# A Fourier mixing and GEGLU kernel on one core: the lone token's products in a tile of their own, and one buffer for folded x

## The chip, the cores and the metric

The kernel runs on one core of a Trainium2 chip. The metric is the device time of one execution in microseconds (us). The engines are named as in the profile: PE is TensorE's matmuls and PEld its weight loads, DVE is VectorE, ACT is ScalarE, POOL is GpSimd, SP is SyncE. Each engine works through its own queue in order; semaphores tie the queues together.

## The reference

```python
def reference(x, w_gate, w_val, w_out):       # x: (8, 3008, 256), d_ff = 1536
    X = np.fft.fft(np.fft.fft(x, axis=1), axis=2).real    # per batch
    X = X.reshape(8 * 3008, 256)
    g = X @ w_gate
    gelu = 0.5 * g * (1.0 + erf(g / sqrt(2)))
    return (gelu * (X @ w_val)) @ w_out
```

All inputs and the output are float32.

## The kernel before

The real part of the transform is built from an even and an odd part over the features, and token t and token T - t share their work. So of the 3008 tokens of a batch only the columns 0 to 1504 (`NCOL` = 1505) are worked through, and each column gives two tokens: a "plus" one and a mirrored "minus" one. Two tokens have no partner of their own, token 0 and token T/2. The latter is called the lone token here.

**Transform.** For each of 8 batches, x comes in by three loads into the tiles `xins`. `fold_x` adds and subtracts mirrored features into the tile xf, 24 pairs of columns wide, in pieces of two columns (two TENSOR_TENSOR and one copy, in the main loop on POOL). `a_step(b, k)` multiplies columns 2k and 2k+1 of xf with the tile G on TensorE. The result goes through DRAM (`z_write`, `z_read`) into Ap, and `b_steps` makes Y from it, with the even part in Y[:, 0] and the odd part in Y[:, 1]. Before, there are two xf tiles, and batch b uses number b % 2.

**Layer 1.** The columns are taken in three chunks, `CH = [(1024, NCOL - 1024), (0, 512), (512, 512)]`, and each chunk in 12 units of 128 features of the hidden layer. So a batch has 36 units, and u counts units over all batches (288). In unit u TensorE makes the gate and value products in PSUM (`ps_g`, `ps_v`). ACT makes gelu of the plus and minus gates (`glp`, `glm`). DVE makes `ev` from each value bank, and for each pair of units the plus products of h (`h<-glp,ps_v`, in `val_odd`), followed by `dv`. POOL makes the minus products of h (`h<-glm,dv`, in `minus`), 128x1024 at a time. In program order the products of a pair are written one unit after its second unit was opened.

**The h buffers.** Each chunk of each batch has an h tile of 12 x 1024 columns, and there are two buffers for it, taken in turn. Chunk 2 of a batch takes the buffer that chunk 0 of that batch had.

**Layer 2.** When a chunk is done, `l2_steps` queues its products with w_out (`ps_o`, TensorE), by windows of 128 tokens. In every following unit, `second` issues eight of them (six in some). `windows` says which columns of h belong to which token rows. When it is called for chunk 0, it also copies 64 left-over columns of h into hx and CW on POOL.

**The lone token.** Its plus products stand in column 960 of chunk 0's h. Its place in the output belongs to a window of chunk 1, column 1023. When the last unit of chunk 1 is done, the line ahead of `l2q += l2_steps(pb, pi)` copies the column from one h tile to the other, on POOL. At that time the buffer's next tenant, chunk 2, has been opened; its first plus products come two units later.

**Order.** Everything is issued in the order in which the Python code runs, engine by engine (`keep_in_program_order`). A unit runs: `val_even`, `gate_minus` and `val_odd` of the unit before, `gate_plus`, steps of the next batch's transform in between (`fills`), `minus`, `fold_x` for the batch after next (for the next one in batch 0's first units), `a_step` for the next batch, and at last `second`. In units 0 to 11 of a batch, `a_step(b + 1, k)` runs in unit k; `fold_x(b + 2, ...)` writes columns 2k and 2k+1 from unit 2k + 5 on. In batch 0 both follow plans of their own (`a_first`, and units 13 to 35).

A tile that is written anew waits for the last readers and writers of what it overwrites; the framework puts in these waits.

Of the kernel before, what the change touches and what calls it, by code (L numbers as in the profile page):

```python
# [10 lines left out]
BF16 = mybir.dt.bfloat16  # L11
# [16 lines left out]
def _sub(base: bass.AP, free_pattern, free_offset, part_start=0, part_num=None):  # L28
    p_step, p_count = base.ap[0]
    if part_num is None:  # L30
        part_num = p_count - part_start
    pat = [[p_step, part_num]] + [list(x) for x in free_pattern]
    off = base.offset + part_start * p_step + free_offset
    return ap_replace(base, ap=pat, offset=off)
# [3 lines left out]
def kernel(  # L38
# [21 lines left out]
    sync, vec, act, pool, pe = (  # L60
        _InOrder(tc, e) for e in (nc.sync, nc.vector, nc.scalar, nc.gpsimd, nc.tensor))
# [5 lines left out]
    HJ = 24  # L67
    NG = 32
    NCH = C // 128
    NFC = F // 128  # L70
# [5 lines left out]
    const_pool = ctx.enter_context(tc.tile_pool(name="const", bufs=1))  # L76
# [20 lines left out]
    NQs = [const_pool.tile([128, YW], BF16, name=f"nq{i}") for i in range(2)]  # L97
    HXF = NFC - NCH * 2
    hx = const_pool.tile([128, HXF, 128], BF16)
    xf_bufs = [const_pool.tile([128, HJ, 2, 128], BF16, name=f"xf{i}") for i in range(2)]  # L100

    Ap = const_pool.tile([128, NG, C], BF16)

# [24 lines left out]
    def S1_tile():  # L128
        return work.tile([128, HJ, C], BF16, tag="S1", bufs=1, name="S1")
# [58 lines left out]
    def ps_o():  # L188
        return psum.tile([128, 512], FP32, tag="o", bufs=1, name="ps_o")

    def ps_d():
        return psum.tile([128, 512], FP32, tag="d", bufs=1, name="ps_d")
# [16 lines left out]

    def fold_x(b, i, eng, a0=0, an=8, other=None):  # L210
        xt = xins[i]
        xf = xf_bufs[b % 2]
        o0 = (8 * i + a0) * C
        lo = _sub(xt, [[C, an], [1, 127]], a0 * C + 1)
        hi = _sub(xt, [[C, an], [-1, 127]], a0 * C + 255)
        ea = _sub(xf, [[C, an], [1, 127]], o0 + 1)
        od = _sub(xf, [[C, an], [1, 127]], o0 + 129)
        eng.tensor_tensor(ea, lo, hi, op=ALU.add)
        eng.tensor_tensor(od, lo, hi, op=ALU.subtract)
        (other or eng).tensor_copy(  # L220
            _sub(xf, [[C, an], [128, 2]], o0), _sub(xt, [[C, an], [128, 2]], a0 * C))
# [239 lines left out]

    def a_step(b, k):

        xf = xf_bufs[b % 2]
        if "S1" not in st[b]:
            st[b]["S1"] = S1_tile()
        S1 = st[b]["S1"]
        if b == 0:
            ps = (ps_g, ps_vh, ps_o if k % 8 < 4 else ps_d, ps_vh)[k % 4]()
        else:  # L470
            ps = ps_o() if b == 1 and k % 2 and 1 < k < 10 else ps_d()
        for i in range(2):
            jj = 2 * k + i
            on_half(ps, pe.matmul(
                ps[:, i * C : (i + 1) * C], G[:, jj, :], _sub(xf, [[1, C]], jj * C),
                start=True, stop=True))
        dst = _sub(S1, [[1, 2 * C]], 2 * k * C)
        if b == 0 and k % 2 == 0 and k >= 8 or b == 1 and k in (0, 3, 5, 7, 9):
            return on_half(ps, vec.tensor_copy(dst, ps))
        return on_half(ps, act.activation(dst, ps, AF.Copy))  # L480
# [92 lines left out]
    hs, banks, duos = {}, {}, {}  # L573
# [93 lines left out]
    def windows(b, ci):  # L667
        h = hs[(b, ci)]
        c0, n = CH[ci]
        m0, nb = c0 // 32, n // 32  # L670
        ps = [plus_rows(b, m0 + i) for i in range(nb)]
        ms = [minus_rows(b, m0 + nb - 1 - i) for i in range(nb)]
        blocks = ps + ms if n == 512 else ms + ps
        order = range(8) if n == 512 else (4, 5, 6, 0, 1, 2, 3)
        out = [(h, 128 * w, blocks[4 * w : 4 * w + 4], None) for w in order]
        if c0 == 0:
            out[-1] = out[-1][:3] + (b * T + T // 2,)
        if len(blocks) % 4:
            left = blocks[-2:]
            o = 64 * (b % 2)  # L680
            pool.tensor_copy(hx[:, :, o : o + 64], h[:, :HXF, 896:960])
            pool.tensor_copy(_sub(CW, [[128, NCH * 2], [1, 64]], o), h[:, HXF:, 896:960])
            if b % 2:
                out.append((None, 0, st[b - 1]["left"] + left, None))
            else:
                st[b]["left"] = left
        return out
# [161 lines left out]
    for u in range(NU + 2):  # L849
        b, i = divmod(u, PER)  # L850
        fills = []
        tail = None
        held = False
        if u < NU:
            open_unit(u)
            loads = (0, 14, 19) if b else (8, 12, 18)
            if i in loads and b + 2 < B:
                load_x(b + 2, loads.index(i))
            if b + 1 < B:
                for what in plan[min(b, 1)].get(i, ()):  # L860
                    if what == "n":
                        tail = lambda b=b: n_step(b + 1)
                        continue
                    eo, q, lo, hi = what
                    if lo == 0:
                        held = True
                        st[b + 1]["cur"] = b_steps(b + 1, eo, q)
                    fills += st[b + 1]["cur"][0][lo:hi]
                    if hi == 8:
                        tail = st[b + 1]["cur"][1]  # L870

        def fill(most=2):
            for _ in range(most):
                if fills:
                    fills.pop(0)()

        def second(n):
            for _ in range(n):
                if l2q:
                    l2q.pop(0)()  # L880

        if u == 0:
            r = banks[0]
            r["pg"] = ps_g()
            layer1(r, r["pv"], WE, 1, 0, r["n"], True)
            layer1(r, r["pg"], WE, 0, 0, r["n"], True)
            layer1(r, r["pg"], WOP, 0, 1, r["n"], False)
            layer1(r, r["pv"], WOP, 1, 1, r["n"], False)
            for e in later_evacs:
                e()  # L890
            n_first(0)
            act.activation(r["glp"][:, : r["n"]], r["pg"][:, : r["n"]], AF.Gelu)
            plus(r)
        elif u < NU:
            val_even(u)
            if not held:
                fill()
        if 0 < u <= NU:
            gate_minus(u - 1)
            if not held:  # L900
                fill()
        early = 0 < u <= NU and banks[u - 1]["kd"]
        if early:
            val_odd(u - 1)
        if 0 < u < NU:
            gate_plus(u, fill)
            if banks[u]["kd"] == 0:
                plus(banks[u])
        if 0 < u <= NU and not early:
            val_odd(u - 1)  # L910
        while fills:
            fill()
        if tail:
            tail()
        if 0 < u <= NU:
            minus(u - 1)
        if u < NU:
            if b + 1 < B and i == (19 if b else 21):
                n_turn(b + 1)
            if b + 1 < B and i == 30:  # L920
                n_read(b + 1)
        if u < NU:
            if b == 0:
                for e in extra.get(i, ()):
                    e()
                if i < 12:
                    fold_x(1, i // 4, pool, i % 4 * 2, 2)
            if i % 2 and b + 2 < B:
                j = i - 1
                if b:  # L930
                    f, fp = next((j - o, n) for n, o, z in ((0, 4, 18), (1, 18, 28), (2, 28, 36)) if j < z)
                else:
                    fp, f = divmod(j - 12, 8)
                if 0 <= f < 8 and fp >= 0:
                    fold_x(b + 2, fp, pool, f, 2)
            if b + 1 < B:
                for k in (i,) if b else a_first.get(i, ()):
                    if k < 12:
                        a_step(b + 1, k)
                        if k in (5, 7, 11):  # L940
                            j0 = {5: 0, 7: 12, 11: 16}[k]
                            z_write(b + 1, j0, 2 * k + 2 - j0)
                    if k in (8, 10, 13):
                        z_read(b + 1, (8, 10, 13).index(k))
        if 0 < u <= NU and u % 12 == 0:
            pb, pi = divmod(u // 12 - 1, 3)
            if CH[pi][0] == 0:
                pool.tensor_copy(hs[(pb, pi)][:, :, 1023:1024], hs[(pb, pi - 1)][:, :, 960:961])
            l2q += l2_steps(pb, pi)
            few = len(l2q) < 96  # L950
        second((6 if few and u % 12 > 5 else 8) if u <= NU else len(l2q))
# [30 lines left out]
```

## Time and profile before

| What | Value |
|---|---|
| median of three runs | 632.25 us |
| the runs | 631.76, 632.25, 635.0 us |
| the profiled execution | 631.74 us |
| its span, first to last instruction | 630.0 us |
| granted TensorE clock, mean | 1.0 |
| POOL copies `h<-h`, 128x12 | 8, each 0.24 us |
| POOL copies `hx<-h` and `CW<-h` | 8 each, 0.60 and 0.39 us |
| POOL folds `xf<-xin`, 128x254 | 168, mean 724 ns |
| POOL products `h<-glm,dv` | 138, mean 2108 ns |

The span is the time between the first and the last instruction that the profiler recorded; the 1.7 us between it and the execution's time lie around it. The rows of the profile name an operation by what it writes and reads, as in `h<-glp,ps_v`, without the numbers of buffers. All rows of the kernel have line L25, since one helper records every operation, so they are told apart by their tiles. "Idle before" in square brackets is the time for which the engine did nothing ahead of a row, with what ended it. Some matmul records are missing from the trace, so that a gap of one matmul's length on PE need not be a stop.

### The profile page before, as it was taken

The numbers are of one execution on the slowest core, as the hardware profiler recorded it, in microseconds if no ns is written. First come the engines' busy times: TensorE is split into PE (matmuls) and PEld (weight loads), VectorE is DVE, ScalarE is ACT, GpSimd is POOL, SyncE is SP. The second block draws the span as 40 slices with busy tenths as digits, with TensorE's granted clock in tenths as the row PEclk, the third lists the DMA queues.
The fourth block names the chain that finished last, engine by engine and source line by source line (L and its number), as shares of the span: only waits on it lengthen the run. The fifth ranks groups of instructions, "written<-read, shape, count | busy, mean of one in ns | idle before, by whom it ended". The sixth has DMA issues, their size and how long they took to land.

```text
span 630.0 us, 12878 instructions
## 1 busy us (share of the span) xinstructions
PE 608.2 (97%) x4522; PEld 402.5 (64%) x4580; DVE 541.7 (86%) x654; ACT 471.8 (75%) x956; POOL 448.7 (71%) x472
## 2 busy tenths in 40 slices
PE   3899999999999999999999999999999999999997
PEld 2445666666666666666666666666666666666665
DVE  7698988898988989888888889889888898999891
ACT  8687778877787777877788777877778777766662
POOL 8396987768868788677777697686885564555452
PEclk9999999999999999999999999999999999999999
DMA  8997423562236512673245532375223611212113
GB/s 313 360 265 247 138 64 114 171 193 90 75 114 207 196 43 75 186 231 102 51 129 177 182 95 76 101 217 192 56 64 97 188 47 44 62 48 52 45 40 84
DMA packets 65458, 82.39 MB, mean 131 GB/s; under 512 B 8298, under 2 KB 58986, under 8 KB 62578
## 3 DMA queue, kind: packets, MB, share of 16 engines
q1 hardware_dynamic: 63682, 80.65, 41.5%
q0 software_dynamic: 1552, 0.79, 0.9%
q8 instruction: 36, 0.59, 0.4%
q14 instruction: 28, 0.23, 0.1%
q10 hardware_dynamic: 160, 0.13, 0.1%
HBM read 45.08 MB, written 37.25 MB: 131 GB/s over the span
## 4 chain that ended last, share of the span: by engine, by line
PE 83%; DVE 9%; POOL 3%; ACT 2%; issue 1%; DMA 1%; SPq 0%; DVEq 0%; ACTq 0%; POOLq 0%
PE ps_o L25 35%; PE ps_g L25 25%; PE ps_v L25 18%; PE ps_d L25 6%; DVE h L25 4%; DVE dv L25 3%; POOL h L25 2%; DVE ev L25 1%; DMA gate<-z 1%; ACT glp L25 1%; DVE S L25 0%; ACT glm L25 0%; ACT S L25 0%; ACT WE L25 0%; DMA out_dram<-osb 0%
## 5 line engine op out<-in xcount | busy, mean ns | idle before, releaser
L25 POOL TENSOR_TENSOR h<-glm,dv 128x1024 bf16<-128x1024 bf16 (+1 forms) x138 | 290.9, 2108 | 157.1 <-DVE dv L25 113.1
L25 PE MATMUL ps_o<-Wo_sb,h 128*128 128x256 bf16 x2136 | 277.7, 272 | 0.4 <-ACT osb L25 0.2
L25 ACT ACTIVATE glm<-ps_g 128x512 bf16<-128x512 f32 (+1 forms) x288 | 169.4, 588 | 111.8 <-PE ps_g L25 75.2
L25 DVE SCALAR_TENSOR_TENSOR ev<-nq,WN,ps_v 128x512 f32<-128x512 bf16 (+1 forms) x276 | 201.9, 734 | 59.0 <-PE ps_v L25 43.4
L25 PEld LDWEIGHTS <-h 128*128 128x128 bf16 x2208 | 210.9, 97 | 54.5 <-issue 0.9
L25 DVE TENSOR_TENSOR h<-glp,ps_v 128x1024 bf16<-128x1024 bf16 (+2 forms) x150 | 173.0, 1153 | 11.1 <-POOL h L25 5.2
L25 ACT ACTIVATE glp<-ps_g 128x512 bf16<-128x512 f32 (+1 forms) x288 | 169.9, 590 | 10.9 <-PE ps_g L25 1.9
L25 DVE SCALAR_TENSOR_TENSOR dv<-ev,ps_v 128x1024 f32<-128x1024 f32 (+1 forms) x138 | 164.8, 1194 | 0.0
L25 POOL TENSOR_TENSOR xf<-xin 128x254 bf16<-128x254 f32 x168 | 118.1, 724 | 0.3 <-DMA xin<-in_x_dram 0.3
L25 PE MATMUL ps_g<-Y,WOM 128*128 128x512 bf16 (+1 forms) x288 | 107.7, 374 | 0.3
L25 PE MATMUL ps_v<-Y,WOP 128*128 128x512 bf16 (+1 forms) x288 | 107.7, 374 | 0.1
L25 PE MATMUL ps_v<-Y,WE 128*128 128x512 bf16 (+1 forms) x282 | 105.7, 375 | 0.9 <-DVE dv L25 0.5
L25 PE MATMUL ps_g<-Y,WOP 128*128 128x512 bf16 (+1 forms) x278 | 103.9, 374 | 1.7
L25 PE MATMUL ps_g<-Y,WE 128*128 128x512 bf16 (+1 forms) x249 | 92.9, 373 | 0.0
L25 PEld LDWEIGHTS <-WOP 128*128 128x128 bf16 x576 | 55.8, 97 | 52.8 <-ACT WOP L25 0.4
L25 PEld LDWEIGHTS <-WE 128*128 128x128 bf16 x576 | 55.9, 97 | 31.5 <-issue 0.9
L25 ACT ACTIVATE osb<-ps_o 128x512 f32<-128x512 f32 x93 | 54.8, 589 | 17.6 <-PE ps_o L25 13.6
L25 PEld LDWEIGHTS <-Ap 128*128 128x128 bf16 (+1 forms) x561 | 40.8, 95 | 35.2 <-issue 1.7
L25 ACT ACTIVATE S<-ps_d 128x512 bf16<-128x512 f32 x80 | 47.4, 593 | 0.1
L25 PEld LDWEIGHTS <-G 128*128 128x128 bf16 x213 | 21.0, 100 | 32.9 <-ACT G L25 8.6
L25 ACT ACTIVATE Y<-ps_d 128x192 bf16<-128x192 f32 (+4 forms) x142 | 34.0, 340 | 0.5 <-PE ps_d L25 0.5
L25 PEld LDWEIGHTS <-WOM 128*128 128x128 bf16 x300 | 29.2, 97 | 5.5 <-issue 0.7
(139 smaller groups left out, 260.8 us busy)
## 6 DMA issues: line engine op xcount, KB each, us to landing
out_dram<-osb SPq DMA_DIRECT2D x358, 64.0 KB
xin<-in_x_dram SPq DMA_DIRECT2D x16, 1024.0 KB
Ap<-z SPq DMA_DIRECT2D x24, 512.0 KB
xin<-in_x_dram SPq DMA_DIRECT2D x8, 896.0 KB
z<-S SPq DMA_DIRECT2D x7, 768.0 KB
z<-S SPq DMA_DIRECT2D x8, 512.0 KB
nq<-nrow SPq DMA_DIRECT2D x8, 376.2 KB
z<-S SPq DMA_DIRECT2D x11, 256.0 KB
```

The lines of the kernel that those rows point to most:

```text
L25: return lambda *a, **k: self._tc.keep_in_program_order(call(*a, **k))
```

## The change

A tile `lone` of 128 x 12 takes the place of the h buffer between the two copies: column 960 of chunk 0's h is copied into it in `windows`, behind the copies into hx and CW, and the later copy into chunk 1's h reads it. That is one more POOL copy in each batch. The two xf tiles become one, which all batches use.

```diff
-    xf_bufs = [const_pool.tile([128, HJ, 2, 128], BF16, name=f"xf{i}") for i in range(2)]
+    xf = const_pool.tile([128, HJ, 2, 128], BF16)
+    lone = const_pool.tile([128, NFC], BF16)
...
     def fold_x(b, i, eng, a0=0, an=8, other=None):
         xt = xins[i]
-        xf = xf_bufs[b % 2]
...
     def a_step(b, k):
 
-        xf = xf_bufs[b % 2]
...
             pool.tensor_copy(hx[:, :, o : o + 64], h[:, :HXF, 896:960])
             pool.tensor_copy(_sub(CW, [[128, NCH * 2], [1, 64]], o), h[:, HXF:, 896:960])
+            pool.tensor_copy(lone, h[:, :, 960:961])
...
             if CH[pi][0] == 0:
-                pool.tensor_copy(hs[(pb, pi)][:, :, 1023:1024], hs[(pb, pi - 1)][:, :, 960:961])
+                pool.tensor_copy(hs[(pb, pi)][:, :, 1023:1024], lone)
             l2q += l2_steps(pb, pi)
```

## The prediction

> **What bounds the kernel now.** I read the page from the top, then the list of waits, the chain that ended last in a stretch of 15 us, and the timeline of that stretch. The page:
>
> ```profile
> PE 608.2 (97%) x4522; PEld 402.5 (64%) x4580; DVE 541.7 (86%) x654; ACT 471.8 (75%) x956; POOL 448.7 (71%) x472
> PE 83%; DVE 9%; POOL 3%; ACT 2%; issue 1%; DMA 1%; SPq 0%; DVEq 0%; ACTq 0%; POOLq 0%
> ```
>
> TensorE is busy for 97% of 630.0 us, most of the remaining 22 us lying in the start and the tail. No speed-up of another engine can give more than the moments at which TensorE still stops. But 12% of the chain runs over DVE and POOL, so such moments exist. The list of waits names candidates:
>
> ```profile
> DVE h L25 <- POOL h L25: 5.2, 7, 0.8
> ...
> DVE h L25 <- PE ps_o L25: 1.0, 1, 1.0
> ...
> PE ps_v L25 <- DVE dv L25: 0.5, 1, 0.5
> ```
>
> Seven waits of DVE for POOL's writes to h, one for each of batches 0 to 6. The eighth (batch 7) is booked on PE: there the DVE row starts at 595.87, when POOL's small copy, 595.60 + 0.24, has just ended. The chain in batch 1:
>
> ```profile
> 153.12 2.15 POOL h L25
> 155.27 0.05 issue
> 155.32 0.25 POOL h L25
> 155.57 0.02 issue
> 155.59 1.22 DVE h L25
> 156.82 1.14 DVE dv L25
> 157.96 0.04 issue
> 158.00 0.38 PE ps_v L25
> ```
>
> and the rows of the timeline around it:
>
> ```profile
> 154.07 0.75 DVE L25 SCALAR_TENSOR_TENSOR ev<-nq,WN,ps_v 128x512 f32<-128x512 bf16 x1 [0.44 <-PE ps_d L25]
> 154.19 0.38 PE L25 MATMUL ps_v<-Y,WOP 128*128 128x512 bf16 x1
> ...
> 154.83 1.04 PE L25 MATMUL ps_o<-Wo_sb,h 128*128 128x256 bf16 x8
> 155.32 0.24 POOL L25 COPY h<-h 128x12 bf16<-128x12 bf16 x1
> ...
> 155.59 1.22 DVE L25 TENSOR_TENSOR h<-glp,ps_v 128x1024 bf16<-128x1024 bf16 x1 [0.78 <-POOL h L25]
> ...
> 156.91 1.03 PE L25 MATMUL ps_o<-Wo_sb,h 128*128 128x256 bf16 x8
> ...
> 158.00 0.38 PE L25 MATMUL ps_v<-Y,WE 128*128 128x512 bf16 x1
> ...
> 159.30 0.93 PE L25 MATMUL ps_o<-Wo_sb,h 128*128 128x256 bf16 x7
> ```
>
> The reader is to see this: POOL's 128x12 copy reads the lone token from the h buffer of chunk 0. The third chunk reuses that buffer, and its first DVE write (155.59) therefore waits for the copy, which stands on POOL behind a 2.15 us product. DVE was free at 154.82 and its matmul had ended at 154.57. DVE then delivers dv late, and the next `ps_v` matmul starts at 158.00.
>
> **What TensorE loses there.** The blocks of eight `ps_o` matmuls give the beat of the units: starts at 150.72, 152.78, 154.83, 156.91, then 159.30. The steps are 2.06, 2.05, 2.08, then 2.39. So 0.34 us is lost: 0.22 between the last `ps_o` matmul and 158.00, the rest before the following `ps_v` matmul, which waits for the late ev. Batches 2 to 6 show the same gaps (0.34 or 0.35 together). In batch 7, where no transform matmuls fill the unit, the beat is 1.95 (594.81 to 596.76) and then 2.82 (to 599.58): 0.87 lost. In batch 0 DVE waits 0.58, but the beat around it is 2.15, 2.16, 2.07, 2.10: nothing lost.
>
> **The change, part by part.**
>
> 1. *The lone token leaves the h buffer early.* The copy into `lone` stands right behind the two copies that `windows` issues (hx, CW), 12 units before the stall. The built program shows the result: the first DVE write to the third chunk's h loses its POOL wait, in all eight batches, and keeps those for PE and ACT, ended at 154.57 and 153.53. It can start at 154.82. The dv behind it gains a POOL wait, for the product two pairs earlier, whose row (148.64 + 2.14) ended five microseconds before that dv. Gain: 6 x 0.34 + 0.87 = 2.9 us. Is something else late next? Advanced by 0.77, dv ends at 157.2 and the ev behind it at 157.9; TensorE is ready for `ps_v` at 157.78 and needs that ev at about 158.3. Both are in time. In batch 7 the shift is 0.97: dv ends near 597.25 and TensorE comes at 597.64; ev ends near 597.9, needed near 598.07.
>
> 2. *The copy it costs.* Eight POOL copies of 128x12, by the row above 0.24 each, 1.9 us of POOL. Behind CW's copy POOL idles for 1.09 to 1.10 us in batches 1 to 7 (131.49 to 132.59 in batch 1) and for 5.3 in batch 0, waiting for DVE's dv. So the idle time hides the copy, and its price is zero. Without that cover, 0.24 on the product behind it would reach DVE only two pairs later. The late copy stays, with the same size; on POOL it still waits for the product before it, but nobody on DVE waits for it any more.
>
> 3. *One xf buffer.* No instruction disappears. POOL's folds gain waits: for PE's matmuls that read the same columns, and in batch 0 for writes of POOL and DVE an earlier batch made. In the built program each awaited matmul stands at least five units (some 10 us) before the fold, because columns 2k and 2k+1 are read in unit k and rewritten from unit 2k+5 on. POOL, itself often waiting for DVE (113.1 us), is never that far ahead. Price: zero. Were the fold held, the product behind it on POOL would be late, and then dv two pairs later.
>
> 4. *More separate wait instructions.* On DVE the built program has 16 more, on POOL 14 more. The nearest rows bound the price: dv with a POOL wait starts 1.13 after its h (150.62 to 151.75), dv without one 1.14 after it (155.59 to 156.73). [...]
>
> 5. *Addresses.* Every tile behind xf moves down by one buffer less the new tile, so h, glm, ev, dv and osb start 32 bytes past a multiple of 64. Y and nq alternate between both kinds of start from batch to batch already: batches 2 and 3 show ev at 745 and 744 ns, and `ps_v` matmuls at 378 to 379 in both. I take zero. The trace does not test the other tiles; that is the slower rival.
>
> **The sum.** The profiled execution took 631.74 us, 630.0 of it span: 631.74 - 2.9 = 628.8. The median of the runs is 632.25, 0.5 above it, so as a median I expect 629.3. The gain is 0.47%; what a measurement of this kernel can tell from no change is about 0.5%, so the forecast lies on that line.
>
> **The rivals.**
>
> *The gap closes only on DVE.* TensorE stops for another reason at the same place, such as the `ps_d` bank that the transform matmuls share, and keeps most of its 0.34. Against: the late rows at 158.00 and 158.66 follow dv and ev directly. If half or less returns, 630.8 to 632.3. Chance 0.09.
>
> *All DVE waiting returns.* 0.58 + 6 x 0.78 + 0.98 = 6.2 us, 626.0. For: the chain follows DVE and POOL for over 7 us in six batches. Against: TensorE kept its beat while DVE waited. Chance 0.04.
>
> *Slower: the new addresses.* One mechanism: TensorE loads h as weights (2208 loads of 97 ns, page) beside `ps_o` matmuls that follow each other every 109 ns (0.87 for eight). If h at its new start loads more slowly, nothing happens up to 109 ns; beyond it, each nanosecond costs 2.2 us, and from 112 ns on the sum turns to slower: 629.3 + 3 x 2.2 = 635.9. For: nothing in the trace shows h there. Against: it takes 15% more per load, and Y, which all matmuls of layer 1 stream, costs the same at both kinds of start. Chance 0.07.
>
> **Numbers.** Forecast 0.80: own range 628.3 to 630.2 (batch 0's 0.58 on top, and run scatter of half a microsecond). A shift of 0.2 us decides whether it reads as over 0.5%: below 629.1 or not. Two of the four executions known of before lie at 631.75 (the others at 632.25 and 635.0); from there the sum is 628.8, 0.55% under the median; I give 0.46 of the 0.80 to faster. Faster: 0.46 + 0.04 = 0.50; same: 0.34 + 0.09 = 0.43; slower 0.07. The range 627.9 to 632.4 takes in the forecast and the first rival, with the scatter on both; 11 in 100 lie outside.
>
> **What would show it.** Right: no DVE wait for POOL h; after the first h write of the third chunk the beat stays at 2.05 (1.95 in batch 7); eight POOL copies into `lone` near 0.24, with idle time behind; folds starting where they did; PE's busy total unchanged and the span 2.9 shorter. Wrong: a wait of PE at the same unit under another name, a `POOL xf` waiting for PE, or longer means in the matmul rows.

## The result and the profile after

The changed kernel takes 0.9964 of the time of the kernel before, with a 95% interval of 0.9953 to 0.9975, 22 executions each. The means are 630.75 and 633.03 us, the medians 630.93 and 632.49. The profiled execution took 629.75 us, 627.6 of it span. The forecast was a median of 629.3 us and a gain of 0.47%; the measured gain is 0.36%. The median lies in the stated range of 627.9 to 632.4, but above the 628.3 to 630.2 that the forecast itself was given. The gain lies on the side of "within 0.5%", to which the prediction gave 0.43.

In about half of the executions of either kernel (11 of 22 of the changed one, 11 of the 25 of the kernel before that ran alongside the first experiments) the mean granted clock is 0.996 or 0.997 and the time about 2 us longer (medians 631.60 against 629.75, and 634.24 against 632.11), so a median depends on how many of them it has (by the medians alone the ratio would be 0.9975), and gains are read below from the units, behind the start. In the four profiles of the first experiments, all with such a mean, TensorE's clock is at 0.50 for 3.4 us in the start.

The page of the changed kernel:

```profile
PE 606.0 (97%) x4522; PEld 402.0 (64%) x4580; DVE 541.5 (86%) x654; ACT 471.8 (75%) x956; POOL 449.7 (72%) x480
PE 91%; DMA 3%; DVE 3%; ACT 1%; issue 1%; POOL 0%; SPq 0%; ACTq 0%; DVEq 0%; POOLq 0%
```

The chain no longer runs over POOL, and DVE's 9% are 3%. DVE's own list of waits, its top rows:

```profile
DVE ev L25 <- PE ps_v L25: 43.5, 89, 1.5
DVE ev L25 <- PE ps_d L25: 18.4, 39, 0.8
DVE osb L25 <- PE ps_d L25: 8.6, 1, 8.6
DVE h L25 <- ACT glp L25: 2.7, 5, 1.0
```

`DVE h <- POOL h` (5.2 us) is gone, and no row has taken its place on the way to h; what grew is DVE waiting for TensorE (`ps_d`, 15.1 to 18.4), which is DVE being early. The timeline of batch 1 at the same place:

```profile
154.60 0.75 DVE L25 SCALAR_TENSOR_TENSOR ev<-nq,WN,ps_v 128x512 f32<-128x512 bf16 x1 [0.44 <-PE ps_d L25]
155.26 1.22 DVE L25 TENSOR_TENSOR h<-glp,ps_v 128x1024 bf16<-128x1024 bf16 x1
155.36 1.04 PE L25 MATMUL ps_o<-Wo_sb,h 128*128 128x256 bf16 x8
155.86 0.24 POOL L25 COPY h<-lone 128x12 bf16<-128x12 bf16 x1
...
156.39 1.22 DVE L25 SCALAR_TENSOR_TENSOR dv<-ev,ps_v 128x1024 f32<-128x1024 f32 x1
...
157.44 1.03 PE L25 MATMUL ps_o<-Wo_sb,h 128*128 128x256 bf16 x8
...
158.31 0.38 PE L25 MATMUL ps_v<-Y,WE 128*128 128x512 bf16 x1
...
159.49 1.04 PE L25 MATMUL ps_o<-Wo_sb,h 128*128 128x256 bf16 x8
```

DVE's h starts at 155.26, right behind ev and 0.60 before POOL's late copy. The blocks of eight `ps_o` matmuls start 2.08 and 2.05 us apart where it was 2.08 and 2.39. The early copy on POOL:

```profile
131.62 0.40 POOL L25 COPY CW<-h 128x256 bf16<-128x256 bf16 x1
131.97 0.20 POOL L25 COPY lone<-h 128x12 bf16<-128x12 bf16 x1
133.12 2.15 POOL L25 TENSOR_TENSOR h<-glm,dv 128x1024 bf16<-128x1024 bf16 x1 [0.96 <-DVE dv L25]
```

It takes 0.20 us, and 0.96 of idle time is left behind it.

**Unit by unit.** I took the start of ACT's `glp` row of every unit in both traces and subtracted. The gain over units 20 to 32 of each batch, where the stall stood, against the kernel before:

| Kernel | Batch 0 | 1 | 2 to 6, each | 7 | Elsewhere, from unit 13 on |
|---|---|---|---|---|---|
| predicted | 0 | 0.34 | 0.34 | 0.87 | 0 |
| the changed kernel | 0.04 | 0.34 | 0.33 | 0.86 | under 0.05 |
| lone tile alone | 0.04 | 0.34 | 0.33 | 0.86 | under 0.05 |
| one xf buffer alone | -0.01 | 0.00 | 0.00 | -0.01 | under 0.05 |

From unit 13 to the end of the span the changed kernel gains 2.92 us. The two profiled executions differ in span by only 2.35, because the one after reached unit 13 0.57 us later.

### The profile page after: what moved, and what is told of

The parts are those of the page before. It is cut to its first block, busy times and chain, and to the rows that moved or that the text cites. A ratio compares the mean times of both kernels' runs of the same rounds, so it can differ in the third digit from the quotient of the medians.

```text
span 627.6 us, 12916 instructions
## 1 busy us (share of the span) xinstructions
PE 606.0 (97%) x4522; PEld 402.0 (64%) x4580; DVE 541.5 (86%) x654; ACT 471.8 (75%) x956; POOL 449.7 (72%) x480
## 4 chain that ended last, share of the span: by engine, by line
PE 91%; DMA 3%; DVE 3%; ACT 1%; issue 1%; POOL 0%; SPq 0%; ACTq 0%; DVEq 0%; POOLq 0%
PE ps_o L25 38%; PE ps_g L25 28%; PE ps_v L25 19%; PE ps_d L25 6%; DMA xin<-in_x_dram 3%; DVE h L25 1%; DVE S L25 0%; DMA z<-S 0%; ACT glp L25 0%; DVE xf L25 0%; ACT glm L25 0%; ACT S L25 0%; POOL xf L25 0%; SPq L25 0%; DVE WOM L25 0%
```

## The experiments

Each experiment's profile is read in the same two ways, by the units and by the time outside the span (time less span). "Full clock" means the executions with a mean granted clock of 0.999 or more.

**One part at a time, and the addresses.** Lone tile alone (on the kernel before):

```diff
+    lone = const_pool.tile([128, NFC], BF16)
...
+            pool.tensor_copy(lone, h[:, :, 960:961])
...
-                pool.tensor_copy(hs[(pb, pi)][:, :, 1023:1024], hs[(pb, pi - 1)][:, :, 960:961])
+                pool.tensor_copy(hs[(pb, pi)][:, :, 1023:1024], lone)
```

> Only the lone tile; the two xf tiles stay. Theory (the whole gain is the released h buffer, one xf buffer is worth nothing): no DVE wait for POOL h, and unit by unit the same lead over the kernel before as in the changed kernel, 0.33 to 0.34 us gained at the third chunk's first h write in batches 1 to 6 and 0.87 in batch 7, 2.9 us in all behind the first unit; time 0.9955 to 0.997 of before. Rival 1 (the lower addresses of the tiles or the single xf buffer bring part of it): under 2 us. Rival 2 (the 0.57 us that the changed kernel's first unit came later belongs to the single xf buffer): here the first unit starts at 28.4 as before, and the span is 627.1.

One xf buffer alone (on the kernel before):

```diff
-    xf_bufs = [const_pool.tile([128, HJ, 2, 128], BF16, name=f"xf{i}") for i in range(2)]
+    xf = const_pool.tile([128, HJ, 2, 128], BF16)
...
-        xf = xf_bufs[b % 2]
```

> Only the single xf buffer; the lone token still goes from h to h. Theory: seven or eight DVE waits for POOL h as before, no change of the beat in any unit, time 0.999 to 1.001 of before. Rival 1 (the folds are held by the transform's matmuls): POOL xf waits for PE in the list of waits, and time above 1.002. Rival 2 (the single buffer costs the start 0.57 us): the first unit's gelu starts near 29.0 instead of 28.4 and the time is 1.001 of before.

Both parts, with 32 unused bytes that put every tile behind them back to a multiple of 64; and the kernel before with the same 32 bytes, which moves its tiles off it:

```diff
+    pad = const_pool.tile([128, 16], BF16)
```

> The changed kernel with an unused tile of 32 bytes behind lone, so that every tile behind it starts at the same place modulo 64 bytes as before. Theory (addresses are worth nothing): same times as the changed kernel, 0.9955 to 0.997 of before, gains by batch of 0.33 to 0.34 and 0.87. Rival (the 0.57 us in the start comes from tiles 32 bytes past a multiple of 64): first unit at 28.4, and 0.001 faster than the lone tile alone without the pad.

> The kernel before with an unused tile of 32 bytes at the same place, nothing else: all tiles behind it start 32 bytes past a multiple of 64. Theory: time 0.999 to 1.001 of before, all matmul, weight load and DVE rows with the same means. Rival (addresses cost, in the start or in the rows): first unit near 29.0, or loads of h above 97 ns; time above 1.001.

| Kernel | Ratio to before, 95% interval | Median at full clock | Outside the span, median |
|---|---|---|---|
| before, run alongside | | 632.11 (14 executions) | 1.79 |
| lone tile alone | 0.9952 (0.9933 to 0.9971) | 629.31 (4) | 2.13 |
| one xf buffer alone | 1.0005 (0.9990 to 1.0019) | 631.68 (5) | 1.78 |
| both, padded | 0.9959 (0.9941 to 0.9976) | 629.30 (3) | 2.17 |
| before, padded | 0.9998 (0.9985 to 1.0011) | 632.35 (6) | 1.78 |

The waits of the kernel with one xf buffer alone, first DVE's, then POOL's, from the lists of each engine:

```profile
DVE h L25 <- POOL h L25: 5.2, 7, 0.8
```

```profile
POOL h L25 <- DVE dv L25: 113.1, 98, 5.5
...
POOL xf L25 <- DMA xin<-in_x_dram: 0.4, 1, 0.4
```

The stall is all there, and no fold waits for TensorE. So the lone tile brings the whole gain. The single xf buffer neither gains nor costs in the units, and its time can't be told from no change (0.9990 to 1.0019). The addresses do not show either: the padded kernel before has `LDWEIGHTS <-h` at 97 ns, ev at 735 ns (734 before) and gains of 0.00 to 0.01 by batch, and the padded changed kernel gains 0.33 to 0.34 and 0.86 like the unpadded one. These four profiles reached unit 13 2.2 to 3.1 us later than that of the kernel before, but all four had the low clock in the start, which the changed kernel's profile had not, so they do not explain its 0.57. The end of TensorE's wait for the gate tile's DMA does: 23.03 us in the kernel before, 23.60 in the changed one, and 23.25 to 23.80 in the five other profiles of kernels with two xf tiles. So 0.57 lies within the start's scatter, and rival 2 of the first expectation has nothing left to stand on.

**How much cover the early copy has.** On the changed kernel:

```diff
-            pool.tensor_copy(lone, h[:, :, 960:961])
+            for _ in range(1 + (0, 0, 3, 8, 16, 24, 32, 40)[b]):
+                pool.tensor_copy(lone, h[:, :, 960:961])
```

> The changed kernel with the early copy into lone repeated, by a different number in each batch: 0, 0, 3, 8, 16, 24, 32, 40 further copies in batches 0 to 7. Each waits for the one before it, so some 0.28 us apiece. Against the changed kernel, unit by unit. Theory (the early copy lies in POOL's idle time and behind it DVE waits only two pairs later, so there is room of about 0.9 us of idle time plus 4.3 us): nothing lost in batches 2 to 4 (0.8, 2.2 and 4.5 us added), 1 to 2 us lost in batch 5 (6.7 added), 3 to 4 in batch 6 and 5 to 7 in batch 7. Rival (only the 0.9 us of idle time is cover, the product behind is on the path): 1.3 us lost in batch 3 and 3.6 in batch 4 already.

Measured against the changed kernel, in one execution: batches 2, 3 and 4 lose 0.00, batch 5 loses 0.58, batch 6 loses 4.6 and batch 7 7.4. Batch 4, with 16 further copies, then the place where batch 5 starts to lose, POOL and DVE:

```profile
355.67 4.37 POOL L25 COPY lone<-h 128x12 bf16<-128x12 bf16 x17
360.00 4.25 POOL L25 TENSOR_TENSOR h<-glm,dv 128x1024 bf16<-128x1024 bf16 x2
```

```profile
437.28 1.22 DVE L25 SCALAR_TENSOR_TENSOR dv<-ev,ps_v 128x1024 f32<-128x1024 f32 x1 [0.92 <-POOL h L25]
```

17 copies cost nothing, so the rival (only 0.9 us of cover) falls: the product behind is late there, by over 3 us, and nobody minds. In batch 5 the wait is the one the prediction named for this case, dv waiting for the late product, two pairs on. That loss came out at half of the least that I expected, for two reasons: the copies took 0.26 us apiece and not 0.28 (16 more in 4.17 us in batch 4), and of DVE's stall of 0.92 TensorE had room for 0.34. The losses of batches 6 and 7 are larger than expected, because TensorE's stops there of 2.7 and 4.6 us come with the low clock (below).

**How much room TensorE has behind DVE's stall.** On the kernel before:

```diff
-                pool.tensor_copy(hs[(pb, pi)][:, :, 1023:1024], hs[(pb, pi - 1)][:, :, 960:961])
+                for _ in range(1 + (4, 0, 1, 2, 3, 4, 6, 1)[pb]):
+                    pool.tensor_copy(hs[(pb, pi)][:, :, 1023:1024], hs[(pb, pi - 1)][:, :, 960:961])
```

> The kernel before with the late copy from h to h repeated: 4, 0, 1, 2, 3, 4, 6, 1 further copies in batches 0 to 7, some 0.29 us apiece, so DVE's stall grows by that. Theory (TensorE has 0.44 us of room behind DVE's stall in batches 1 to 6 and about 0.1 in batch 7, and beyond it loses one for one): lost per batch 0.34 with 0 further copies, 0.63 with 1, 0.92 with 2, 1.2 with 3, 1.5 with 4, 2.1 with 6; batch 7 1.16; batch 0 with 4 about 1.1. Rival (TensorE loses a share of the stall, 0.34 of 0.78): 0.47, 0.6, 0.72, 0.85, 1.1 in the same order.

Batch 5, with 4 further copies, in the timelines of POOL, DVE and PE:

```profile
454.58 1.44 POOL L25 COPY h<-h 128x12 bf16<-128x12 bf16 x5
```

```profile
456.05 1.22 DVE L25 TENSOR_TENSOR h<-glp,ps_v 128x1024 bf16<-128x1024 bf16 x1 [1.98 <-POOL h L25]
```

```profile
456.17 1.03 PE L25 MATMUL ps_o<-Wo_sb,h 128*128 128x256 bf16 x8
458.46 0.38 PE L25 MATMUL ps_v<-Y,WE 128*128 128x512 bf16 x1 [1.25 <-DVE dv L25]
```

| Batch | Further copies | DVE's stall | Lost against the kernel before | Theory: 0.29 each | Rival: a share of the stall |
|---|---|---|---|---|---|
| 1 | 0 | 0.77 | 0.0 | 0 | 0 |
| 2 | 1 | 1.08 | 0.31 | 0.29 | 0.13 |
| 3 | 2 | 1.38 | 0.60 | 0.58 | 0.26 |
| 4 | 3 | 1.69 | 0.92 | 0.86 | 0.38 |
| 5 | 4 | 1.98 | 1.20 | 1.16 | 0.51 |
| 6 | 6 | 2.58 | 3.48 | 1.76 | 0.76 |
| 7 | 1 | 1.28 | 0.30 | 0.29 | not given |
| 0 | 4 | 1.78 | 1.20 | about 1.1 | not given |

(One execution. The expectation's figures less the kernel before's 0.34, and less 0.87 in batch 7.) Beyond its room TensorE loses one for one; the room is 0.44 us in batches 1 to 6, 0.11 in batch 7 and 0.58 in batch 0, where a stall of 0.58 therefore cost nothing. Batch 6 lost 1.7 more than the theory and 2.7 more than the rival: TensorE stood for 1.85 us, and soon behind that the granted clock was 0.50 from 534.76 to 538.18 us. At half the clock these 3.4 us hold, as an estimate, the work of 1.7, which is the difference. So the low clock is not a matter of the start alone.

**The start's low clock.** On the changed kernel:

```diff
-    warm(4)
+    warm(13)
     warm(8, gate[:, :])
```

> The changed kernel with 13 instead of 4 idle matmuls in the start, ahead of those that wait for the gate tile's DMA, so that TensorE stays busy until 23.0 us. Other runs of both kernels show a granted clock of 0.50 for about 3 us behind that wait, where TensorE had stood for 2.3 us or more, and a time about 2 us longer. Theory (standing still brings the low clock on): no execution below a mean clock of 0.998, all times near 629.3, median 0.9945 to 0.996 of before. Rival (the low clock comes by itself): the share of executions with a mean clock of 0.996 or 0.997 stays near one half and the ratio near 0.996. What may go wrong: the matmuls of the gate start later than the DMA lands, by up to 0.2 us.

The windows from 18 to 24 and 24 to 30 us, columns as on the heading line (PE busy first, PEclk third from the end), of the padded changed kernel, whose profiled execution had the low clock, and of this one:

```profile
core 0: us, PE busy (x) PEld busy (x) DVE busy (x) ACT busy (x) POOL busy (x), PEclk, DMA share, GB/s
18.00:24.00 6.00, 3.49 (x15) 1.30 (x15) 4.85 (x25) 3.84 (x10) 0.00 (x0) 1.00 1.03 325
24.00:30.00 6.00, 6.00 (x103) 3.93 (x102) 2.61 (x12) 2.69 (x7) 3.12 (x3) 0.72 0.99 384
```

```profile
18.00:24.00 6.00, 5.46 (x25) 2.27 (x25) 4.84 (x25) 3.84 (x10) 0.00 (x0) 1.00 1.00 332
24.00:30.00 6.00, 6.00 (x113) 4.00 (x111) 3.08 (x13) 4.03 (x11) 3.20 (x3) 1.00 1.02 407
```

With idle matmuls in the gap TensorE stands for 0.26 us, where it stood for 2.34 in the padded kernel, and the clock stays at 1.00. All six executions had a mean clock of 0.999 or 1.0 (629.25 to 630.40, median 629.81), against 11 of 22 of the changed kernel. The ratio to before is 0.9948 (0.9933 to 0.9964). At full clock its median, 629.81, is that of the changed kernel, 629.75, so the longer warm-up saves what the low clock cost and nothing else. Six executions alone would leave some doubt; the six of the last experiment make it twelve of twelve.

**What lies outside the span.** In the first table the kernels with the lone tile spend 0.35 us more outside the span. The changed kernel (2.15), the one with the longer warm-up (2.13) and the one with 123 more early copies (2.15, one execution) do so too; the one with 21 more late copies does not (1.82, one execution). The programs of the two groups differ on DVE, 959 instructions against 943, by the 16 additional wait instructions (the traces hold 957 and 941 of them). So the kernel before got more DVE instructions of another kind, two fills a batch, and in a second kernel eight (`range(8)`):

```diff
+    pad = const_pool.tile([128, 16], BF16)
...
             pool.tensor_copy(_sub(CW, [[128, NCH * 2], [1, 64]], o), h[:, HXF:, 896:960])
+            for i in range(2):
+                vec.memset(pad[:, i : i + 1], 0.0)
```

> The kernel before with 16 more instructions on DVE: two 128x1 fills of an unused tile in each batch, issued where the hx and CW copies are. Open is why kernels with the lone tile spend 2.13 to 2.15 us outside the span (time less span) and those without it 1.78 to 1.82. The programs of the two groups differ on DVE: 959 instructions against 943, the 16 additional wait instructions. Theory (the count of DVE's instructions matters, whatever they do): about 2.15 us outside the span here. Rival (it is something else of the lone tile): about 1.8 us. The beat of the units should not change, nothing in the span beyond the scatter of the start.

> The same with 64 more instructions on DVE, eight fills in each batch. Theory in its linear form (22 ns for each instruction): about 3.2 us outside the span. Theory in its step form (a boundary is crossed between 943 and 959): about 2.15 us. Rival: about 1.8 us.

With 16 more (959 instructions) the median outside the span is 2.14 us (2.11 to 2.24, 8 executions), with 64 more (1007) it is 1.79 (1.73 to 1.87, 8 executions); the kernel before, run alongside, 1.79 (1.73 to 1.83, 15 executions). The ratios are 1.0005 (0.9984 to 1.0026) and 0.9983 (0.9967 to 0.9999); the second lies below 1 because 6 of 8 executions were at full clock, against 6 of 15 of the kernel before (medians at full clock 632.2 and 632.4). In the units the 16 fills cost nothing and the 64 cost 0.2 us in batch 7, where nothing was expected. So the time outside the span goes with the number of DVE's instructions, not with what they do, and it neither grows with the number nor is it a boundary passed once. Why 959 is dear and 943 and 1007 are not stays open.

**Both remedies at once.** The kernel with 13 warm matmuls, and 48 fills on DVE behind its last dv, where it waits 8.6 us for TensorE, so 1007 instructions:

```diff
+        if u == NU:
+            for j in range(48):
+                vec.memset(pad[:, j % 16 : j % 16 + 1], 0.0)
         second((6 if few and u % 12 > 5 else 8) if u <= NU else len(l2q))
```

> The changed kernel with 13 idle matmuls in the start and 48 fills of an unused tile on DVE in the tail, where DVE waits 8.6 us for the last matmuls: 1007 DVE instructions as in the kernel with 64 more, where 1.79 us lay outside the span. Theory (the place of DVE's last instructions decides, and the lone tile itself has no price there): 1.8 us outside the span instead of 2.15, a median near 629.4 and no execution below a mean clock of 0.998; ratio 0.994 to 0.9955. Rival (something of the lone tile costs there too): 2.15 us outside.

Outside the span it has 1.79 us (1.73 to 1.91), so the lone tile has no price of its own there. Six executions of 628.83 to 630.09 us, median 629.55, none below a mean clock of 0.999; ratio to before 0.9945 (0.9926 to 0.9963). Its lead over the kernel with 13 warm matmuls alone, 0.3 us, is within the scatter.

## Why the prediction was right, and where a term was off

*The stall and its eight places* were right: DVE's first write of chunk 2 waited for POOL's late copy in all batches, batch 7 included, which the list of waits booked on PE. *The gain by units*, 6 x 0.34 + 0.87 = 2.9, was measured as 0.34 + 5 x 0.33 + 0.86 and 0.04 in batch 0, with 2.92 us in all. The first rival (half or less of it) and the second (6.2 us) fall with that. It held because the beat of the `ps_o` blocks was taken, and not the 6.2 us of DVE's waiting or the 2.3% of POOL in the chain: the doses show 0.44 us of room between the two. *Nothing late next*: right, by the list of waits and the beat.

*The early copy's price of zero* was right (0.20 us, 0.96 idle behind it, 17 in a row still free). *The single xf buffer at zero* was right by the run that had it alone, and *the addresses at zero* by the two padded runs; the slower rival has no row to stand on, with h's loads at 97 ns at either start.

*The additional wait instructions* (step 4), for which the sum has no term, were what was mis-sized. Inside the span they are indeed free, with no loss in any unit. But the step stopped at the span, and the sum carried 1.74 us around it over unchanged; it became 2.15. The trace of before could not show this, since it lies ahead of the first or behind the last instruction. No run shows a price of the 16 in the beat, and the 0.35 outside comes with plain fills too.

So 2.9 less 0.35 is about 2.55 us, 0.40%, inside the measured interval. At full clock the median after is 629.75 (632.11 before, in the first experiments), 0.45 above the forecast and inside its own range. The median of all executions, 630.93, lies another 1.2 higher through the start's low clock in half of them, which the prediction has no term for; the three times known of before had it, to judge by the time, in one (635.0). That 630.93 lies in the stated range is luck: that part of the range was there for the first rival, which did not come. The chance of 0.50 for "faster by over 0.5%" was too high; it leaned on the sum's place at the line, and 0.35 us was enough to move it.

## What to carry to other kernels

A buffer that is taken in turn is held by its last reader, however small: a copy of 12 elements behind a 2.15 us product held 24 KB per partition and cost 2.9 us in a kernel whose bounding engine was 97% busy. Look, at the place where a buffer gets its next tenant, for late readers of a few columns, and read them out early into a tile of their own. Size such a gain by the beat of the engine that bounds the kernel, not by the waiting of the engine that is held: up to its room (0.44 us here) the wait costs nothing, and beyond it one for one.

## What the runs showed of the hardware that was not expected

TensorE's granted clock falls to 0.50 for 3.4 us behind stops that I had thought harmless, and the length of the stop alone does not decide. In the profiles, stops of 1.85, 2.24, 2.25, 2.31, 2.34, 2.56, 2.70, 2.94 and 4.57 us were followed by it (the last one for 6.83 us); stops of 1.78, 2.00, 2.10 and 2.30 were not. In the trace of the cover experiment the clock is at 0.50 from 24.55 to 27.97, from 516.07 to 519.49 and from 591.16 to 597.99 us.

Two stops of nearly the same length, at the same place: 2.34 us, up to 23.58, in the padded changed kernel, and 2.30, up to 23.60, in the changed kernel, columns as in the table of windows above:

```profile
22.00:24.00 2.00, 0.42 (x2) 0.21 (x3) 1.16 (x6) 1.98 (x7) 0.00 (x0) 0.99 1.02 316
24.00:25.00 1.00, 1.00 (x4) 0.37 (x3) 0.53 (x1) 1.00 (x1) 0.00 (x0) 0.50 0.79 277
25.00:26.00 1.00, 1.00 (x4) 0.37 (x3) 0.00 (x0) 0.24 (x2) 0.00 (x0) 0.50 1.04 377
26.00:27.00 1.00, 1.00 (x11) 0.52 (x10) 0.00 (x0) 0.00 (x0) 0.33 (x1) 0.50 1.09 416
27.00:28.00 1.00, 1.00 (x38) 1.00 (x35) 0.78 (x5) 0.46 (x2) 0.79 (x2) 0.81 1.05 436
```

```profile
22.00:24.00 2.00, 0.40 (x2) 0.21 (x3) 1.16 (x6) 1.98 (x7) 0.00 (x0) 1.00 1.04 353
24.00:25.00 1.00, 1.00 (x6) 0.48 (x5) 0.58 (x1) 1.00 (x1) 0.00 (x0) 1.00 0.98 342
25.00:26.00 1.00, 1.00 (x29) 0.76 (x28) 0.23 (x1) 0.33 (x3) 0.00 (x0) 1.00 1.00 377
26.00:27.00 1.00, 1.00 (x39) 0.91 (x35) 1.00 (x7) 0.99 (x4) 0.50 (x1) 1.00 1.14 449
27.00:28.00 1.00, 1.00 (x32) 0.81 (x27) 0.44 (x4) 0.41 (x1) 0.80 (x2) 1.00 1.05 442
```

The first was followed by 0.50, behind the second the clock stayed at 1.00. What decides besides the length was not shown; the traces were made for other questions.

And the number of DVE's instructions alone moved 0.35 us outside the span, up at 959 (2.14 us) and down again at 1007 (1.79, as at 943).
